# A windowed-attention and gated-MLP kernel on one core: q and k in one transfer each, heads paired two apart, other accumulator banks for the third chunk, another instruction order

## The chip, the cores and the metric

The kernel runs on one core of one Trainium2 chip. The core has TensorE (PE in the profile, with PEld for its weight loads), VectorE (DVE), ScalarE (ACT), GpSimd (POOL) and SyncE (SP), whose queue issues nearly all transfers, and 16 DMA engines that carry them. Sums of matmuls lie in eight banks of the PSUM memory, everything else on the chip in SBUF. The metric is the device time of one execution in microseconds (us).

## The reference

Four batches, eight heads, 768 positions and a head size of 64; attention sees 8 global positions and the last 96, with a bias that falls with distance. Its output, as 3072 rows of 512, goes through an MLP with 2048 hidden columns and the activation h·tanh(softplus(h)).

```
scores = scale * np.matmul(q, k.transpose(0, 1, 3, 2))
rel = pos[:, None] - pos[None, :]
is_global = pos[None, :] < int(n_global)
is_local = (rel >= 0) & (rel < int(n_local))
dist = np.where(is_global & ~is_local, float(n_local), np.abs(rel))
scores = scores - slopes[:, None, None] * dist
scores = np.where(is_global | is_local, scores, -1e9)
a = softmax(scores)
x = (a @ v), heads side by side, 3072 x 512
h = x @ w_in
g = h * np.tanh(np.where(h > 20.0, h, np.log1p(np.exp(np.minimum(h, 20.0)))))
out = g @ w_out
```

## The kernel before

The tokens are cut into 12 **chunks** of 256 (three to a batch), each chunk into two blocks of 128. The heads are worked in two sets of four, so there are 24 **groups** (two to a chunk): group G holds q and k of four heads of chunk G/2. For each group the kernel loads q (tile qr, 128 rows, 2 × 256) and the keys that the window sees (tile kr, 128 rows, 2 × 416): 64 rows for one head of a pair, 64 for the other. Attention in the first three chunks is computed in 32-bit floats (CF32 = 3). In the later ones, and in the MLP throughout, each operand is split into two 16-bit floats whose products are added.

The instructions of all engines come from one string, PROGRAM. A token is a letter and a number; the loop calls the letter's function with the number, and each engine, and each queue, runs its share of the calls in that order. A mark (') moves the operation to another engine (VectorE in place of ScalarE or of GpSimd). The letters that matter here:

- q: `load_qk`, loads of group G (L163 on). v, x: loads and copies of values (vo, vc). w: loads of weights of the MLP (wts, wr).
- s: scores (L407), one call for two pairs of heads, so group G is used by s4G and s4G+2. t: their maxima on VectorE (L421). y: exponentials on ScalarE (L430).
- P: the probabilities are turned by TensorE in the first three chunks (L460) and F copies them out (tile AT). In later chunks X turns them by a transposing transfer on SP's queue (L450).
- W: the probabilities weigh the values (L482, L486). R and what follows: the rows are normalised, turned (O, U or the transfer V) and split.
- A, S, B, C, D, E: the weights of the MLP are split into two 16-bit parts.
- i: layer 1 (L549), 8 blocks to a chunk, so i0 to i95. j, u, n, r, G, H, z, Z: its activation. o: layer 2 (L605). Q, Y: output. L, M: masks.

PSUM's eight banks go by name: two for scores (sc), two for layer 1 (ph), two for layer 2 (po0, po1) and two for the sums of weighed values (pav0, pav1). Before the change, `turn_p` puts the turned probabilities of chunk 2 in the ph banks (those of chunks 0 and 1 in po), and `weigh` puts all sums in pav.

In `load_qk` q is one transfer per group from qT, 128 rows of 2 × 256. k is two transfers of 64 rows from kd, one to each head of the pairs. In the first chunk of a batch only the last 288 of the 416 columns are loaded (144 KB each in place of 208 KB). For group 0 the second half of k is issued on ScalarE's queue, everything else on SyncE's. The tiles qr and kr have three buffers each, so the load of a group waits until the one three loads back is converted or used.

Of the kernel before, what the change touches and what calls it, by code (L numbers as in the profile page):

```python
# [114 lines left out]
def windowed(st, tc, loc):  # L115
# [47 lines left out]
    def load_qk(G):  # L163
        if G >= 2 * NC:
            return
        ci, g = divmod(G, 2)
# [5 lines left out]
        nc.sync.dma_start(qr, L.qT[b].rearrange("(a j) d s -> (j d) a s", j=2)[:, pairs, c * CH:(c + 1) * CH])  # L172
# [469 lines left out]
    def checks(i):  # L642
# [40 lines left out]
        R2 H0 P17 s18 O2 W15 W14 y16 A4 F17 z0 t19 y19 C7 t18 T2' U2 E3 E1 Z0 P16 s20 P19 C4 t20 B6 t21 y18 F19 y20 F16' D4' E4' S5' A5 B12 R3 B5 o0 P20 P18
        s22 y21 F20 S12 A12 W17 O3 S6 T3 F18 A6 A8 C5 D7' t22 U3 W19 W20 P21 i8 E7 B8 C6 C12 t23 S8' D6' y22 F21 y23 j8 D5 E6 G8 E5' C8 B13 B10 S13' W21 P23
        W18 W16 P22 F22' R4 F23 u8 n8 S10 D12 r8 A13 D8 W23 i1 i9 w16 w11 E12 E8 H8 j1 A10 u1 S9 z8' C13 G1 j9 O4 W22 A14' Z8' C10 D10' R5 o8 u9 n1 n9 r1 r9
        T4 A15 S14 A11 E10 G9 A9' D13' E13 H1 U4 B14 i2 i10 z1 B9 C14 B15 B11 H9 Z1 S11 j2 z9 C11 C9 G2 h3' Z9' j10 u10 n10 D9 D11 r10 D14 u2 n2 S15' G10
        E9' S16' C15 H10 z10' r2 D15 A16 E14 w18 w24 w22 w21 w20 w17 w25 q6 w19 w26 Z10 H2 E11' o1 o9 i3 o10 O5 B16 S18 C16 A18 z2 j3 E15 Z2 u3 A17 n3 T5
        S17 A20 S20' r3 D16' G3 A24 B18 B17 U5 E16' B20 C18 B24 C17 D17 H3 o2 i11 i16 j11 z3 S24 G11 D18' E18 i12 w28 q7 w23 u11 J16 A22 n11 r11 Z3 C20 D20
        j12 A25' B19 E17 H11 S22' G12 A19 z11 C24 Z11' o3 i4 i17 D24 B22 E24 C22 E20 S19 u12 j4 D22 u4 n4 c7 n12 G4 S25' C19 B25 a7' C25 d7' b7 o11 s24 i18
        D19 r12 J17 r4 E22' H4 N0 t24 D25' A26' H12 t25 z4' J18 y25 A21 z12 E25' l3 E19' Z12' S26' B21 B26 Z4' i13 s26 i5 o12 j13 y24 G13 u13 S21 j5 A28 o4  # L690
        i20 q9 w30 w27 S28' C21 C26 D26' E26' B23 B28 t26 A30 u5 n5 D21 C28 g25 r5 n13 B30 G5 J20' S30' g24 E21' y26 r13 A23 H5 S23' i19 i6 p25' z5 A27 C23
        J19' D23 E23' c8' C30 H13 j6 u6 D28 g26 z13 B27 p26' Z5 Z13' D30' G6 E28' E30 p24 d8 w29 X25 w31 v4 X24 q8 x3 X26 i14 o5 i21 j14 u14 n6 r6 n14 S27
        r14 G14 H6 t27 S31 a8 i7 C27 y27 J21 z6 j7 u7 D27 B29 b8 S29' E27 Z6' H14 z14 Z14 i15 s28 o13 o14 o6 n7 r7 j15 u15 a9 n15 A31' A29' B31 G7 H7 t28
        C29 C31 G15 D31' z7' Z7' r15 D29 j16 u16 j17 y28 u17 n17 n16 r16 g27 H15 g28' p28' G16 z15' t29 E29 E31 H16 Z15 z16' G17 p27' Z16' o7 s30 o15 j18
# [4 lines left out]
        z24 o23 i27 W33 W32 s38 i26 y36 n25 r25 j27 g34' p34' h5' g37 u27 Q2 j26 a12 b11 Z24' H25 G27 g36' t39 p37' z25' p36 Z25 t38 G26 y39 n27 r27 y38 u26
        X34 q12 X37 q14 X36 o24 o25 W35 s40 i28 i29 W34 W37 g39 n26 r26 p39 H27 t40 H26 z26' c12' Z26' z27' t41 l5 j28 u28 g38 n28 Z27 d12 p38 G28 r28 y40  # L700
        j29 u29 n29 X39 x5 X38 W39 o26 o27 s42 W36 W38 i30 H28 G29 y41 r29 z28 H29 a13' g40' R8 T8' g41' p41' t43 j30 c13 p40 Z28 X40 U8 b12 o28 R9 z29 V8
        u30 Z29 t42 T9 G30 y43 v6 d13 U9 i31 n30 r30 g43' V9 p43' H30 s44 X41 j31 z30' o29 u31 t45 X43 n31 G31 r31 y45 q15 H31 i32 z31' t44 Z30' Y2 b13 q13
        o30 j32 y42 g42 g45' p45' G32 h6' X45 u32 p42' i34 n32 a15' l6 y44 r32 g44' x6 s46 j34 W43 t47 W40 y47 i33 H32 X42 t46 u34 y46 Z31' z32' c14' n34
        Z32 o31 p44' j33 u33 Q3 g47' p47' W41 G34 s48 X44 G33 n33 W45 o32 r33 r34 H33 z33' g46' Z33 t49 i36 H34 t48 d14 z34 p46' y49 Z34' X46 o33 j36 y48
        G36 X47 g49' u36 p49 n36 o34 r36 a14 H36 g48' s50 i35 i37 j35 z36 G35 u35 b14 Z36 n35 t51 r35 i38 p48 y51 H35 z35' j37 t50 Z35 u37 G37 y50 W44 g51'
        W46 R10 s52 n37 W47 j38 W42 T10' o35 X49 r37 U10 H37 V10 p51' z37 t52 c15 Z37 o36 a16' v7 u38 X51 n38 R11 r38 X48 G38 o37 T11' U11 H38 V11 b15 d15'
# [188 lines left out]
```

## Time and profile before

| | us |
|---|---|
| median of 3 runs (lowest to highest) | 622.98 (621.86 to 624.29) |
| the profiled execution, its own time | 621.52 |
| the profiled execution, span of its trace | 619.7 |
| VectorE busy | 463.2 |
| ScalarE busy | 444.8 |
| GpSimd busy | 163.3 |

The costliest groups of the page (line, engine, operation, out<-in, count, busy time and mean of one, and the idle time before them with what ended it):

```profile
L549 PE MATMUL ph<-xT,wts 128*128 128x256 f16 x2304 | 263.6, 273 | 0.2 <-POOL wts L154 0.2
...
L605 PE MATMUL po<-wts,gt 128*128 128x512 f16 x1056 | 238.7, 379 | 0.8 <-DVE gt L148 0.5
```

The two layers of the MLP take 502.3 of TensorE's busy time; the rest is attention. "Busy" counts an engine's instructions only, so the wait for a transfer shows as idle time of the engine that waits, with the releaser's name behind the arrow. A transfer's row gives the time at which it was issued, and the page's list of issues the time from there to landing.

### The profile page before, as it was taken

The numbers are of one execution on the slowest core, as the hardware profiler recorded it, in microseconds if no ns is written. First come the engines' busy times: TensorE is split into PE (matmuls) and PEld (weight loads), VectorE is DVE, ScalarE is ACT, GpSimd is POOL, SyncE is SP. The second block draws the span as 40 slices with busy tenths as digits, with TensorE's granted clock in tenths as the row PEclk, the third lists the DMA queues.
The fourth block names the chain that finished last, engine by engine and source line by source line (L and its number), as shares of the span: only waits on it lengthen the run. The fifth ranks groups of instructions, "written<-read, shape, count | busy, mean of one in ns | idle before, by whom it ended". The sixth has DMA issues, their size and how long they took to land.

```text
span 619.7 us, 13567 instructions
## 1 busy us (share of the span) xinstructions
PE 603.1 (97%) x5066; PEld 417.0 (67%) x5066; DVE 463.2 (75%) x1198; ACT 444.8 (72%) x1106; POOL 163.3 (26%) x135
## 2 busy tenths in 40 slices
...
DMA  8998465235365859226357554474374344320001
GB/s 222 285 264 280 142 201 150 71 110 133 69 142 132 161 103 217 53 63 144 69 90 196 100 129 103 102 176 62 68 160 83 65 71 105 87 35 1 34 2 38
DMA packets 123014, 73.02 MB, mean 118 GB/s; under 512 B 91712, under 2 KB 112192, under 8 KB 122944
## 3 DMA queue, kind: packets, MB, share of 16 engines
q1 hardware_dynamic: 122800, 71.97, 49.8%
...
q10 hardware_dynamic: 144, 0.15, 0.1%
...
## 4 chain that ended last, share of the span: by engine, by line
PE 77%; DVE 11%; ACT 4%; issue 4%; DMA 2%; SPq 0%; POOL 0%; DVEq 0%; ACTq 0%; POOLq 0%
PE ph L549 33%; PE po L605 30%; PE sc L407 5%; PE pav L486 3%; PE pav L482 2%; DVE gf L587 2%; DVE gf L583 2%; DMA wts<-w_in 1%; DMA AT<-hl 1%; DVE ws L357 1%; PE po L460 1%; DVE A L421 1%; ACT A L430 1%; PE pav L605 1%; DVE ws L353 1%
## 5 line engine op out<-in xcount | busy, mean ns | idle before, releaser
L549 PE MATMUL ph<-xT,wts 128*128 128x256 f16 x2304 | 263.6, 273 | 0.2 <-POOL wts L154 0.2
L549 PEld LDWEIGHTS <-wts 128*128 128x128 f16 x2304 | 222.8, 98 | 35.5 <-issue 1.9
L605 PE MATMUL po<-wts,gt 128*128 128x512 f16 x1056 | 238.7, 379 | 0.8 <-DVE gt L148 0.5
L605 PEld LDWEIGHTS <-gt 128*128 128x128 f16 x1152 | 110.1, 98 | 126.8 <-issue 2.9
L154 POOL TENSOR_TENSOR gt<-gf,gt 128x512 f16<-128x512 f32 x55 | 67.5, 1229 | 278.7 <-DVE gt L148 142.7
L567 ACT ACTIVATE e<-ph 128x512 f32<-128x512 f32 x90 | 53.1, 590 | 89.9 <-PE ph L549 89.7
L430 ACT ACTIVATE A<-A,nm 128x256 f32<-128x256 f32 (+1 forms) x192 | 91.6, 478 | 29.1 <-DVE nm L421 29.1
L587 DVE CUSTOM_DVE_ANT_0 gf<-gf,u 128x512 f32<-128x512 f32 x96 | 79.5, 829 | 42.9 <-ACT u L579 41.7
L583 DVE SCALAR_TENSOR_TENSOR gf<-e,ph 128x512 f32<-128x512 f32 x90 | 61.1, 682 | 52.4 <-ACT e L567 51.3
L421 DVE CUSTOM_DVE_ANT_0 A<-sc,mb 128x256 f32<-128x256 f32 (+1 forms) x192 | 68.3, 396 | 16.9 <-PE sc L407 13.8
L154 POOL TENSOR_TENSOR hl<-A,hl 128x512 f16<-128x512 f32 (+1 forms) x36 | 44.8, 1250 | 74.2 <-DVE hl L148 31.8
L571 ACT ACTIVATE u<-e 128x512 f32<-128x512 f32 x96 | 59.9, 625 | 1.7
L579 ACT ACTIVATE u<-u 128x512 f32<-128x512 f32 x96 | 59.4, 624 | 1.8
L575 ACT ACTIVATE u<-u 128x512 f32<-128x512 f32 x96 | 59.5, 623 | 1.7
L154 POOL TENSOR_TENSOR wts<-ws,wts 128x512 f16<-128x512 f32 x20 | 25.7, 1292 | 72.1 <-ACT wts L150 37.6
L150 ACT ACTIVATE gt<-gf 128x512 f16<-128x512 f32 x44 | 27.4, 623 | 22.0 <-DVE gmax L587 22.0
L430 ACT ACTIVATION_READ_ACCUMULATOR A<-A,nm 128x1 f32 x192 | 36.0, 188 | 0.0
L486 PEld LDWEIGHTS <-AT 128*128 128x128 f16 x792 | 28.7, 98 | 7.2 <-issue 1.9
L154 DVE TENSOR_TENSOR hl<-A,hl 128x512 f16<-128x512 f32 (+1 forms) x36 | 30.0, 834 | 2.0 <-ACT hl L150 1.7
L154 DVE TENSOR_TENSOR gt<-gf,gt 128x512 f16<-128x512 f32 x41 | 28.9, 706 | 3.3 <-ACT gt L150 2.9
L407 PE MATMUL sc<-wc,ws 64*128 64x256 f16 (+1 forms) x432 | 28.2, 262 | 0.7 <-DVE nm L421 0.7
L486 PE MATMUL pav<-vo,AT 128*128 128x64 f16 x432 | 27.5, 193 | 0.0
...
## 6 DMA issues: line engine op xcount, KB each, us to landing
kr<-kd SPq DMA_DIRECT2D x32, 208.0 KB, 4.2
qr<-qT SPq DMA_DIRECT2D x24, 256.0 KB, 4.2
wts<-w_in SPq DMA_DIRECT2D x12, 512.0 KB, 8.3
wts<-w_out SPq DMA_DIRECT2D x12, 512.0 KB, 8.9
out<-ob SPq DMA_DIRECT2D x11, 512.0 KB, 3.8
vr<-v SPq DMA_DIRECT2D x9, 512.0 KB, 5.1
...
kr<-kd SPq DMA_DIRECT2D x15, 144.0 KB, 5.1
```

The costliest lines, as they stand in the source:

```text
L154: (nc.vector if other else nc.gpsimd).tensor_tensor(out, in_, high, op=ALU.subtract)
L407: nc.tensor.matmul(sc[j][:, a2, 0:w], x[half, a2, rows_], y[half, a2, col0:col0 + w], start=(n == 0), stop=(n == len(terms) - 1))
L421: nc.vector.tensor_tensor_reduce(out=A[:, j, 0:w], in0=sc[j][:, 0:w], in1=m, scale=-1.0 / (UNIT if ci < CF32 else UNIT * SQ), scalar=3.0e3 ...
L430: nc.scalar.activation(A[:, j], A[:, j], AF.Exp, bias=nm[:, h:h + 1], scale=-1.0, accum_out=rs[:, h:h + 1])
L486: nc.tensor.matmul(pav[:, cols], AT[:, (x * 2 + j) * nk + kk, :], vs[kk][:, y, cols], start=(n == 0), stop=(n == last))
L549: nc.tensor.matmul(ph[:, j, :].rearrange("p (b t) -> p b t", b=2), wv4[:, 2 * fb, x, c * P:(c + 1) * P], xT[:, :, y * NCC + c, :], start=( ...
L571: nc.scalar.activation(u, mish[m]["e"], AF.Square, bias=0.5)
L575: nc.scalar.activation(mish[m]["r"], mish[m]["u"], AF.Ln, bias=0.25 / RS, scale=1.0 / RS)
L579: nc.scalar.activation(r, r, AF.Exp, scale=-1.0)
L583: nc.vector.scalar_tensor_tensor(gf, mish[m]["e"], 0.5, mish[m]["h"], op0=ALU.add, op1=ALU.mult)
L587: nc.vector.tensor_tensor_reduce(out=gf, in0=gf, in1=mish[m]["r"], scale=SG / (SV * SW * RS), scalar=0.0, op0=ALU.mult, op1=ALU.max, accum ...
L605: nc.tensor.matmul(pos[ci][t], gt[:, x, j, t * P:(t + 1) * P], wv4[:, 2 * fb + 1, y, :], start=(fb == 0 and n == 0), stop=(fb == NFB - 1 a ...
```

## The change

1. `load_qk`: q and k of a group are each one transfer, written as a pattern of three loops: 2 half sets, 64 rows, and one run of 2 heads × 256 (or 416) columns. All 416 columns are loaded in every chunk. k of group 0 goes on ScalarE's queue. q now comes from qd, which is laid out as kd is.
2. The rows of a half set belong to heads h and h+1; a pair on TensorE's upper and lower rows is now h and h+2 (`head`).
3. The copy of the far values to vc (32 rows) is one transfer in place of two in chunks 1 and 2.
4. No mask is made on GpSimd.
5. `turn_p` puts the turned probabilities of chunk 2 in the scores' banks (sc) in place of layer 1's (ph), and `weigh` puts the sums of chunk 2 in layer 1's banks in place of pav. `turn_x32` uses sc for chunk 2.
6. PROGRAM has the same tokens in another order up to about i30 and z31, 230 us into the trace before; behind that only a few tokens move by a place or two.

```
-        pairs = slice(g * GH // 2, (g + 1) * GH // 2)
...
-        nc.sync.dma_start(qr, L.qT[b].rearrange("(a j) d s -> (j d) a s", j=2)[:, pairs, c * CH:(c + 1) * CH])
-        for j in range(2):
-            half = slice(j * D, (j + 1) * D)
-            (nc.scalar if G == 0 and j else nc.sync).dma_start(kr[half, :, o:], L.kd[ci, half].rearrange("p (a j) w -> p a j w", j=2)[:, pairs, j, o:])
+        for dst, src, w, queue in ((qr, L.qd, CH, nc.sync), (kr, L.kd, KW, nc.sync if G else nc.scalar)):
+            both = bass.AP(src.tensor, ci * P * H * w + g * GH * w, [[D * H * w + GH // 2 * w, 2], [H * w, D], [1, GH // 2 * w]])
+            queue.dma_start(dst.rearrange("p a w -> p (a w)"), both)
...
+    def head(g, a2, j):
+        return g * GH + j * (GH // 2) + a2
...
-                for t in range(2):
-                    nc.sync.dma_start(vc[NPREV:P, t], far)
+                nc.sync.dma_start(vc[NPREV:P], far.unsqueeze(1).broadcast_to([NGMAX, 2, DM]))
...
-        if other and h >= H // 2:
-            nc.gpsimd.tensor_scalar(out, in_, -L.slopes[h] * UNIT, None, op0=ALU.mult)
-        else:
-            copy(out, in_, -L.slopes[h] * UNIT, other)
+        copy(out, in_, -L.slopes[h] * UNIT, other)
...
-            h = g * GH + 2 * a2 + j
+            h = head(g, a2, j)
...
-        turn = ps.tile([P, 2, CH], F32, name="ph") if t >= 2 * 8 else ps.tile([P, DM], F32, name=f"po{t % 2}", bufs=1).rearrange("p (j t) -> p j t", j=2)
+        turn = ps.tile([P, 2, W], F32, name="sc") if t >= 2 * 8 else ps.tile([P, DM], F32, name=f"po{t % 2}", bufs=1).rearrange("p (j t) -> p j t", j=2)
...
-            pavs[ci, blk] = ps.tile([P, DM], F32, name=f"pav{blk}", bufs=1)
+            if ci == 2:
+                pavs[ci, blk] = ps.tile([P, 2, CH], F32, name="ph").rearrange("p j t -> p (j t)")
+            else:
+                pavs[ci, blk] = ps.tile([P, DM], F32, name=f"pav{blk}", bufs=1)
...
-        turn = ps.tile([P, 2, CH], F32, name="ph").rearrange("p j t -> p (j t)").rearrange("p (k t) -> p k t", t=P)
+        turn = (ps.tile([P, 2, CH], F32, name="ph") if n < 4 else ps.tile([P, 2, W], F32, name="sc")).rearrange("p j t -> p (j t)").rearrange("p (k t) -> p k t", t=P)
...
-        I0 K0 L2 K1 L4 L0 L3 v0 w2 q1 x0 s0 t1 y1 M3 P1 L1' t0 s2 B2 F1' f0 M0 M2 M1 L5 y0 A2 t3 t2 P0 W1 y3 P3 q2 w0 v1 w1 q3 x1 s4 F0' M6' M4' M7' L7' M5'
+        I0 K0 s0 w2 v0 q1 w0 x0 q2 w1 K1 L0' L1 L3 t1 M5 y1 L2' t0 L6 M2 M7 L5 M4 L7 y0 M1 M0 M3' f0 B2 A2' P1 s2 F1' S2' C2 P0 W1 t3 t2 y3 F0' P3 s4 A0'
```

What that does to the engines' orders at three places. First SyncE's queue at the start of the program; n_i is the pair of window sizes, vo and vc are values, wts weights. Before:

```order
L62 DMA n_i<-n 128x4
L172 DMA qr<-qT 128x2x256
L175 DMA kr<-kd 64x2x288
L209 DMA vo<-v 128x2x512
L322 DMA wts<-w_in 128x4x256
L172 DMA qr<-qT 128x2x256
L175 DMA kr<-kd 64x2x288 x2
L229 DMA vc<-v 96x512
```

and with the change:

```order
L62 DMA n_i<-n 128x4
L171 DMA qr<-qd 128x1x512
L317 DMA wts<-w_in 128x4x256
L208 DMA vo<-v 128x2x512
L171 DMA qr<-qd 128x1x512
L171 DMA kr<-kd 128x1x832
L317 DMA wts<-w_in 128x4x256
L228 DMA vc<-v 96x512
```

The first weights (token w2) are issued ahead of the values, q and k are one row each of 128 rows (the shape is the tile's), and a second load of weights stands ahead of the copies to vc.

Second, SyncE's queue in chunks 4 and 5, some 200 us into the trace, where q12, q14 and q15 are loaded between the transposing transfers of probabilities (AT) and of rows of x (xT). Before, with q12 and q14 as the two loads of q:

```order
L450 DMA_TRANSPOSE AT<-hl 128x8x128
L172 DMA qr<-qT 128x2x256
L175 DMA kr<-kd 64x2x288 x2
L450 DMA_TRANSPOSE AT<-hl 128x8x128
L172 DMA qr<-qT 128x2x256
L175 DMA kr<-kd 64x2x416 x2
L450 DMA_TRANSPOSE AT<-hl 128x8x128 x2
```

and with the change, with q12, q14 and q15:

```order
L445 DMA_TRANSPOSE AT<-hl 128x8x128 x2
L171 DMA qr<-qd 128x1x512
L171 DMA kr<-kd 128x1x832
L445 DMA_TRANSPOSE AT<-hl 128x8x128
L530 DMA_TRANSPOSE xT<-xhl 128x8x128
L171 DMA qr<-qd 128x1x512
L171 DMA kr<-kd 128x1x832
L208 DMA vr<-v 128x2x512
L530 DMA_TRANSPOSE xT<-xhl 128x8x128
L445 DMA_TRANSPOSE AT<-hl 128x8x128 x2
L171 DMA qr<-qd 128x1x512
L171 DMA kr<-kd 128x1x832
```

The loads of groups 12 and 14 have moved behind the transposes X39 and X38 (the first row) and X40, so that they stand close to that of group 15.

Third, VectorE ahead of the first maxima of chunk 0's second block (tile A from sc, token t3); fl are flags of the window sizes, ws and wc parts of weights. Before:

```order
L353 TENSOR_SCALAR ws_172<-wts_99 128x512
L148 TENSOR_SCALAR AT_174<-po1_159 128x256
L626 TENSOR_SCALAR fl_105<-n_f_62 1x1
L627 TENSOR_SCALAR fl_105<-n_f_62,fl_105 1x1
L628 TENSOR_SCALAR fl_105<-n_f_62,fl_105 1x1
L629 TENSOR_SCALAR fl_105<-n_f_62,fl_105 1x1
L421 ISA A_190,nm1_189<-sc_166,mb_97 128x256
```

and with the change:

```order
L627 TENSOR_SCALAR fl_105<-n_f_62,fl_105 1x1
L348 TENSOR_SCALAR ws_181<-wts_99 128x512
L148 TENSOR_SCALAR wc_183<-wts_99 128x512
L148 TENSOR_SCALAR AT_194<-po1_185 128x256
L342 TENSOR_SCALAR ws_181<-wts_99 128x512
L352 SCALAR_TENSOR_TENSOR ws_181<-wc_183,ws_181 128x512
L416 ISA A_206,nm1_205<-sc_188,mb_97 128x256
```

Three more operations on the first weights stand ahead of the maxima on VectorE, and the flags ahead of them all.

More of the change, by code (lines that the diff above doesn't have):

```diff
@@ L476, in weigh @@
         for j in range(2):
-            h = g * GH + 2 * a2 + j
+            h = head(g, a2, j)
             cols = slice(h * D, (h + 1) * D)
@@ L556, in hold_h @@
         if k < 2:
-            if k == 0:
+            if "h" not in obs:
                 obs["h"] = mt.tile([P, 2, DM], F32, name="ob", bufs=1)
@@ L683, in windowed @@
[L683 to L694, printed above, removed]
@@ L699, in windowed @@
[L699 to L706, printed above, removed]
@@ L719, in windowed @@
-        Z59' X72 W70 j61 W71 o59 u61 G61 a24 H60 g75 R17 X73 n61 r61 p75' i62 z60' T17' Z60 H61 z61' Z61 s76 j62 o60 u62 G62 n62 r62 a22 H62 W72 W73 t77 o61
-        z62 h10' Z62 U17 t76 i63 V17 y76 l10 X75 b24 o62 j63 u63 n63 g74 g76' p76 d21 G63 y77 i65 p74' g77 r63 p77 H63 X77 i64 j65 q22 z63 u65 Z63' X74 s78
-        j64 o63 u64 G64 X76 G65 n64 n65 t78 r65 y78 H65 W77 i66 r64 H64 t79 y79 z64' W75 g78' W74 Z64 Q7 s80 W76 p78 t81 i67 j66 y81 R18 u66 T18' c22 z65'
-        o64 Z65' n66 j67 G66 t80 u67 n67 U18 o65 b22 r67 V18 r66 G67 g79' X78 p79' H66 i68 X79 z66' g81' Z66 H67 v11 d22' p81 W78 j68 o66 u68 n68 X81 z67 Y7
@@ L723, in windowed @@
-        s82 x10 W79 t82 a23 i69 y82 Z67' r68 g82' G68 y80 t83 o67 H68 R19 z68 j69 Z68 T19' u69 s84 n69 G69 o68 r69 U19 g80 b23 V19 y83 p82' p80' X82 i70 t85
-        y85 t84 X80 H69 c24 g85' z69' i71 j70 Z69 u70 G70 h11' n70 r70 o69 H70 j71 z70' g83' Z70 p85 s86 o70 p83 X83 t86 y86 d24' W81 u71 W82 G71 X85 i74
-        n71 c23' y84 d23 r71 i73 j74 u74 G74 H71 n74 t87 r74 i72 g84' j73 z71' p84 u73 n73 Z71 X84 r73 g86 s88 j72 p86 o71 t88 u72 H74 y87 G73 g87 t89 y88
-        p87 W84 H73 W80 W83 z74' n72 W85 X87 r72 Z74' i75 G72 X86 g88' H72 p88' s90 j75 X88 i76 u75 t91 t90 R20 W87 z73' z72 y89 Z72 Q8 o72 T20 Z73 y91 n75
@@ new lines, in windowed @@
+        F3' L4 y2 t4 t5 y5 y4 P2 W3 s6 F2' S0' M6' B0 t6 w3 v1 q3 x1 P4 W2 P5 W0 t7 A1' S1' C0 B1 F4 y6 F5 y7 P6 s8 W4 P7 W5 t8 t9 R0 C1 F6 y8 F7 y9 D2 W6
+        s10 P8 P9 W7 O0 t11 t10 D1 F8' A3' E1' R1 y11 y10 F9 T0 D0 S3 E2 E0 s12 W8 P11 O1 W9 P10 w7 w13 q4 w24 w8 w6 q5 w12 v2 w4 w5 w11 w10 x2 w14 t13 t12
+        T1' B3 U1 U0 y13 F11 y12 F10 s14 P13 i0 P12 A7 F13 S13 t14 S7' B7 C3 B13 t15 C7 F12' y14 y15 W13 s16 W12 P15 P14 W11 W10 j0 G0 S6 u0 A13 n0 r0 D7'
+        D3' t17 R2 H0 z0' t16 B6 A6 F15 F14 y17 y16 O2 W15 W14 P17 P16 E3 E7 Z0 F17 T2 A4 F16 R3 O3 o0 s20 T3 C13 C6 B4 S4' U2 C4 U3 D6 D4 i8 E4' t20 D13'
@@ new lines, in windowed @@
+        S28 S27' C27 Z13' B28 C28 i6 i20 w30 q8 X25 w31 q9 w29 X24 X26 J20' j6 n5 j16 A30 c8 r5 u6 D27 S30' B30 G6 g27' d8' H5 C30 a8' b8 D28' z5' o13 i14
+        i21 s28 j14 n6 u14 n14 Z5 E27 u16 r6 D30 r14 n16 G14 J21' r16 t29 E28' H6 y29 z6' H14 Z6 E30 o5 i19 i7 z14 S31 t28 J19 y28 S29 G16 B29 H16 z16 j7
+        j17 u7 n7 r7 u17 n17 o6 s30 i15 Z16 B31 A29' Z14' C29 D29' g28' G7 E29' g29' A31' a9' r17 C31 H7 z7 j15 D31 u15 c9 n15 r15 G17 Z7' E31 o14 o7 p27'
+        b9 G15 H17 H15 z15' d9 t30 Z15' p28' Q0 j19 j18 u18 y30 u19 o16 o15 X27 x3 Y0 n18 r18 Q1 n19 r19 p29' z17' Z17' G18 t31 H18 z18' Z18 g30' G19 H19
@@ new lines, in windowed @@
+        j20 a10 y31 u20 n20 j21 u21 r20 z19' l4 Z19' c10' G20 G21 p30 o17 W25 s32 W26 W24 o18 i22 q10 X28 X29 X30 W28 W29 W27 t32 H20 g31 n21 z20 r21 p31'
+        R6 H21 z21' Z21' t33 T6 Z20 U6 q11 X31 o19 i23 W30 W31 s34 o20 o21 j22 R7 T7' j23 u23 u22 n22 y32 r22 U7 g32' G22 t34 d10 p32 b10 t35 n23 y33 y34
+        g34 g33 r23 G23 p34' H23 z23' H22 z22' Z22 p33 V6 V7 X33 Y1 X32 x4 v5 X34 i24 s36 i25 j24 u24 G24 t36 Z23 n24 j25 u25 n25 r24 y36 y35 r25 G25 t37
+        H24 c11' o22 o23 s38 i26 W32 i27 W33 g35 Q2 j26 j27 u26 d11 n26 a11 r26 y37 g37 z24' p35' g36' t39 H25 z25' p36 Z24 a12' Z25' t38 G26 G27 H26 c12'
@@ new lines, in windowed @@
+        h5 u27 y38 y39 z26' d12' l5 b11 Z26' p37 X36 X35 X37 x5 o24 o25 i28 W35 s40 W36 W34 o26 W37 i29 g39 j28 u28 g38 n27 r27 H27 z27 n28 p39 p38 Z27 X39
+        X38 q12 r28 t40 G28 b12 y40 j29 t41 R8 H28 z28 g40' p40' G29 T8 u29 Z28' o27 W39 s42 W38 i30 o28 U8 t43 c13' y41 a13 n29 r29 j30 H29 z29' u30 g41'
+        Z29 p41 R9 X40 V8 q14 v6 T9 d13 y43 t42 i31 G30 n30 U9 r30 g43' V9 p43' s44 H30 j31 X41 z30' o29 u31 t45 n31 X43 G31 r31 y45 H31 q15 i32 z31' t44 Y2
+        Z30' b13 q13 o30 j32 y42 g42 g45' p45' G32 X45 h6' u32 p42' i34 n32 a15' l6 y44 r32 g44' x6 s46 j34 W43 t47 W40 y47 i33 H32 X42 t46 u34 y46 Z31'
@@ new lines, in windowed @@
+        z32' c14' n34 Z32 o31 p44' j33 u33 Q3 g47' p47' W41 G34 s48 X44 G33 n33 W45 o32 r33 r34 H33 z33' g46' Z33 t49 i36 H34 t48 d14 z34 p46' y49 Z34' X46
+        o33 j36 y48 G36 X47 g49' u36 p49 n36 o34 r36 a14 H36 g48' s50 i35 i37 j35 z36 G35 u35 b14 Z36 n35 t51 r35 i38 p48 y51 H35 z35' j37 t50 Z35 u37 G37
+        y50 W44 g51' W46 R10 s52 n37 W47 j38 W42 T10' o35 X49 r37 U10 H37 V10 p51' z37 t52 c15 Z37 o36 a16' v7 u38 X51 n38 R11 r38 X48 G38 o37 T11' U11 H38
+        V11 b15 d15' i39 t53 y53 z38' g50' b16 p50 s54 j39 i40 u39 G39 Z38 X50 y52 n39 q16 r39 H39 W49 Y3 o38 z39' t55 Z39 y55 c16 o39 j40 d16 g53 G40 g52
@@ new lines, in windowed @@
+        X64 y68 G55 p67' y69 X67 s70 z54 W66 t71 c20 Z54 i56 v9 g68' g69 H55 p69' z55 o54 Z55 j56 u56 d19 n56 h9' r56 d20 o55 G56 t70 y70 b21 p68' Q6 i57
+        H56 X68 g70 z56 X69 W67 j57 s72 i58 u57 t72 G57 n57 Z56' r57 b20 y71 H57 W64 j58 W68 z57' i59 g71 G58 Z57 u58 l9 p70 p71' W69 j59 o56 u59 X70 n58
+        t73 G59 n59 X71 r58 R16 y72 o57 Y6 T16' g72 y73 x9 g73' H58 q21 s74 z58 i60 Z58 t75 v10 p73' q23 p72 o58 j60 u60 G60 c21' n60 t74 r59 y75 i61 H59
+        U16 r60 z59' V16 y74 Z59' X72 W70 j61 W71 o59 u61 G61 X73 a24 H60 g75 R17 n61 r61 p75' i62 z60' T17' Z60 H61 z61' Z61 s76 j62 o60 u62 G62 n62 r62
@@ new lines, in windowed @@
+        a22 H62 W72 W73 t77 o61 z62 h10' Z62 U17 t76 i63 V17 y76 l10 X75 b24 o62 j63 u63 n63 g74 g76' p76 d21 G63 y77 i65 p74' g77 r63 p77 H63 X77 i64 j65
+        q22 z63 u65 Z63' X74 s78 j64 X76 o63 u64 G64 G65 n64 n65 t78 r65 y78 H65 W77 i66 r64 H64 t79 y79 z64' W75 g78' W74 Z64 Q7 s80 W76 p78 t81 i67 j66
+        y81 R18 u66 T18' c22 z65' o64 Z65' n66 j67 G66 t80 u67 n67 U18 o65 b22 r67 V18 r66 G67 g79' X78 p79' H66 i68 X79 z66' g81' Z66 H67 v11 d22' p81 W78
+        j68 o66 u68 n68 X81 z67 Y7 s82 x10 W79 t82 a23 i69 y82 Z67' r68 g82' G68 y80 t83 o67 H68 R19 z68 j69 Z68 T19' u69 s84 n69 G69 o68 r69 U19 g80 b23
```

58 lines of the change are left out of this document (28 added, 30 removed).

## The prediction

> **What bounds the kernel now.** I read the busy table first, then the chain of work that ended last, then the busy slices, then the stretches, and last the transfers. The page of the profile:
>
> ```profile
> PE 603.1 (97%) x5066; PEld 417.0 (67%) x5066; DVE 463.2 (75%) x1198; ACT 444.8 (72%) x1106; POOL 163.3 (26%) x135
> ...
> DMA  8998465235365859226357554474374344320001
> ...
> q1 hardware_dynamic: 122800, 71.97, 49.8%
> ...
> PE 77%; DVE 11%; ACT 4%; issue 4%; DMA 2%; SPq 0%; POOL 0%; DVEq 0%; ACTq 0%; POOLq 0%
> ```
>
> TensorE is busy for 603.1 of 619.7 us, and it is most of the chain. So the kernel runs at the length of its matmuls, and a change can save at most the 16.6 us in which TensorE stands still. It can lose any amount, if something makes TensorE wait. The DMA row says where that could come from: in the first 60 us, and again in three or four bursts, the 16 engines are nearly full. The stretches show it in numbers (columns: stretch, length, busy time of PE, PEld, DVE, ACT and POOL, granted clock, DMA share, GB/s):
>
> ```profile
> 0.00:20.00 20.00, 11.85 (x78) 8.77 (x80) 12.52 (x61) 11.90 (x43) 4.82 (x12) 1.00 0.92 252
> 80.00:100.00 20.00, 19.20 (x138) 13.26 (x137) 19.09 (x31) 16.76 (x34) 9.28 (x7) 1.00 0.47 145
> 160.00:180.00 20.00, 19.24 (x190) 12.15 (x189) 19.26 (x48) 18.48 (x50) 6.17 (x5) 1.00 0.61 125
> 180.00:200.00 20.00, 19.11 (x133) 11.85 (x130) 17.78 (x45) 12.90 (x34) 3.96 (x3) 1.00 0.56 128
> ...
> 20.00:40.00 20.00, 20.00 (x170) 17.19 (x169) 18.60 (x68) 19.08 (x60) 4.49 (x4) 1.00 1.07 258
> 21.00:25.00 4.00, 4.00 (x35) 3.56 (x36) 3.81 (x18) 3.68 (x13) 0.00 (x0) 1.00 1.06 243
> 48.00:50.00 2.00, 2.00 (x13) 1.10 (x12) 1.97 (x7) 2.00 (x8) 0.00 (x0) 1.00 1.04 385
> 53.00:55.00 2.00, 2.00 (x20) 2.00 (x19) 2.00 (x8) 1.76 (x4) 1.17 (x1) 1.00 0.95 359
> ```
>
> Half of TensorE's idle time lies before 20 us (20 − 11.85 = 8.15). After that it never waits long, with VectorE busy nine tenths of the time beside it. Where the DMA share is 1, all 16 engines move 243 to 385 GB/s together. One engine's rate is therefore 385/(16 × 1.04) = 23.1 GB/s at 48 to 50 us, 359/(16 × 0.95) = 23.6 at 53 to 55, and 243/(16 × 1.06) = 14.3 at 21 to 25, where the 64-row halves of k travel.
>
> **The loads of q and k.** Which transfers there are, with their size and the time from issue to landing:
>
> ```profile
> kr<-kd SPq DMA_DIRECT2D x32, 208.0 KB, 4.2
> qr<-qT SPq DMA_DIRECT2D x24, 256.0 KB, 4.2
> wts<-w_in SPq DMA_DIRECT2D x12, 512.0 KB, 8.3
> ...
> kr<-kd SPq DMA_DIRECT2D x15, 144.0 KB, 5.1
> ...
> vc<-vc SPq DMA_DIRECT2D x12, 64.0 KB, 2.6
> ```
>
> 256 KB in 4.2 us is 62 GB/s with the latency counted in, more than two engines' worth: before, a load of q is spread widely. Every transfer of before starts its pattern with a loop over 32, 64, 96 or 128 rows. The new pattern of q and of k starts with a loop over 2 (two half sets of heads), with 64 rows below it, and ends in one run of 2 or 3.25 KB. How many engines share such a transfer is the **unknown of this change**, and no row of before shows it. The ends are 16 engines, as for all transfers so far, and two, one to each step of the outer loop. An even share needs a loop that it can be cut along, and the outermost loop is the one that all the transfers of before have with a count of 16 or more. I take the cut along it, so two engines, and the same two each time.
>
> The Trainium skill, page "DMA: Bandwidth & Descriptors", section "Why a DMA increments its semaphore by 16 and not by 1", has a rule for this: a transfer goes over the largest number of engines, up to 16, that divides the slowest loop (of size above 1) of both patterns, and the hardware queues use the lowest-numbered engines. Here that is two, always the same; the trace neither confirms nor denies it. It speaks against this change and for my choice.
>
> With two engines a group's 256 + 416 KB = 688,128 bytes take 344,064/23.1 = **14.9 us**. At 14.3 GB/s they would take 24.1.
>
> **The start.** Where the first groups are needed (columns: start, length, engine, line, operation):
>
> ```profile
> 1.20 0.42 SPq L172 DMA_DIRECT2D qr<-qT  x1
> ...
> 6.06 1.22 PE L407 MATMUL sc<-kr,qr 64*128 64x128 f32 x8 [6.06 <-DMA kr<-kd]
> ...
> 7.11 0.43 DVE L279 SCALAR_TENSOR_TENSOR e<-e 128x256 f32<-128x256 f32 x1
> ...
> 7.46 0.28 DVE L421 CUSTOM_DVE_ANT_0 A<-sc,mb 128x128 f32<-128x128 f32 x1
> ...
> 10.75 0.55 DVE L353 TENSOR_SCALAR ws<-wts 128x512 uint16<-128x512 uint16 x1 [2.14 <-DMA wts<-w_in]
> ...
> 45.48 1.14 PE L407 MATMUL sc<-kr,qr 64*128 64x256 f32 x8
> ```
>
> The last row is token s20, the first scores of group 5. Groups 0 to 5 are 6 × 14.9 = 89.4 us on each of the two engines. On SP's queue eleven transfers of 512 KB and the transfers for x0 and x1 (about 0.75 MB) stand ahead of group 5 or among them. Spread over 16 engines, each of the eleven takes 524,288/16/23.1 = 1.42 us, and all of this 15.6 + 2.1 = 17.7 us. With 3 us until the first bytes flow, group 5 is there at 89.4 + 17.7 + 3 = 110.1 us, and s20 is **64.6 us** late. Everything on TensorE stands in program order behind it. The new order puts some matmuls ahead of s20 and takes others away, which could give back 2 or 3 us; I leave that out. The first scores come at 17 to 20 us instead of 6.06.
>
> **Later.** After the start there are 18 groups for some 500 us, so single loads of 14.9 us hide, and bursts don't:
>
> ```profile
> 220.02 5.30 SPq L450 DMA_TRANSPOSE AT<-hl  x2
> ...
> 235.75 0.58 SPq L172 DMA_DIRECT2D qr<-qT  x1
> ...
> 238.49 0.41 SPq L172 DMA_DIRECT2D qr<-qT  x1
> ...
> 402.36 0.72 SPq L172 DMA_DIRECT2D qr<-qT  x1
> ...
> 405.15 0.47 SPq L172 DMA_DIRECT2D qr<-qT  x1
> ...
> 431.46 0.58 SPq L172 DMA_DIRECT2D qr<-qT  x1
> ```
>
> ```profile
> 250.81 0.26 PE L486 MATMUL pav<-vc,AT 128*128 128x64 f16 x3
> ...
> 419.93 0.51 PE L486 MATMUL pav<-vo,AT 128*128 128x64 f16 x12
> ...
> 439.92 0.25 PE L486 MATMUL pav<-vc,AT 128*128 128x64 f16 x3
> ...
> 484.85 0.83 PE L407 MATMUL sc<-wc,ws 64*128 64x256 f16 x12
> ```
>
> In the new order q12 and q14 are issued behind the transposes X39 and X38 (the row at 220.02, until 225.3), with q15 and q13 close behind (235.75 and 238.49) and then X45. Four groups are 59.6 us, so X45 comes out of the engines at 225.3 + 59.6 = 284.9, and its weighing W45 stood at 250.81: **+34.1**. Groups 21 and 23 (402.36 and 405.15) push X72 to 402.36 + 29.8 = 432.2, against W72 at 419.93: **+12.2**. Group 22 pushes X74 to 431.46 + 14.9 = 446.4, against W74 at 439.92: **+6.4**. If the transposes pass the loads, only the scores of group 13 are late, by 14 us.
>
> A check without any single wait: queue q1 holds each engine for 0.498 × 619.7 = 309 us. About 41 of these (15.1 MB/16/23.1) are q and k; in their place come 24 × 14.9 = 358. The two engines then have 626 us of work, more than the whole span, and up to group 22's load:
>
> ```profile
> 0.00:431.50 431.50, 420.90 (x3572) 295.25 (x3573) 356.49 (x925) 328.60 (x833) 120.76 (x101) 1.00 0.59 141
> ```
>
> 0.59 × 431.5 = 255, less 41, plus 358, is 572 us before q22 has landed, while s88, its first user, stood at 484.85. So +87 at the least if the two engines hold all of it, and some +75 if q and k held 53 instead of 41.
>
> **The other parts.** *Fewer issues:* 48 for q and k instead of 72, each near 0.6 us of SP by the rows above; SP isn't waited for, so nothing, either way. *Heads h and h+2 paired:* the same instructions on other columns, nothing. *Banks:* chunk 2's probabilities now turn in the scores' banks and its sums lie in layer 1's. That frees the two sum banks earlier for layer 2 of chunk 1. In return the next scores wait for the copy out of the bank:
>
> ```profile
> L148 DVE TENSOR_SCALAR gt<-gf 128x512 f16<-128x512 f32 x15 | 7.2, 481 | 0.3
> ...
> L148 DVE TENSOR_SCALAR AT<-po 128x512 f32<-128x512 f32 x6 | 4.1, 684 | 0.8 <-PE po L460 0.8
> ```
>
> Eight turns by 0.684 us, all uncovered, would be +5.5. The best case is that the gaps in 80 to 100, 160 to 180 and 180 to 200 us (0.80 + 0.76 + 0.89) go: −2.4. I take 0, since TensorE is at 20.00 of 20.00 in the stretch beside them. *The order of weights and masks:* masks leave POOL, and three more operations on weights (near 0.5 us each by the gt row: some 1.5 us) now stand before the second block's maxima on VectorE, which in return need not wait 2.14 us for w2. That cancels to within 1 us.
>
> **Rivals.**
> 1. *Sixteen engines, nothing gained.* The loads take 4 to 8 us as before. Having q and k sooner buys nothing, as VectorE makes the masks until 7.54 (7.11 + 0.43) and takes its first maximum at 7.46 already. VectorE, at 0.89 to 0.99 of its time, sets the pace until 200 us. 621.5, or with its extra conversions up to 624. For it: all transfers of before do spread. Chance 0.10.
> 2. *Sixteen engines and faster.* One mechanism: VectorE's wait of 2.14 us at 10.75 goes, and the freed banks fill the 2.4 us of gaps: 621.5 − 2.1 − 2.4 = 617. It decides where the loads of group 0 land before 6 us; then VectorE's queue, not the transfers, sets the start. Chance 0.09.
> 3. *A small split, but on changing engines,* so that groups run beside each other. Only the first scores wait, 17 to 20 instead of 6.06, and the bursts vanish: 621.5 + 12 = 634. Nothing in the profile says that the engines change. Chance 0.05.
>
> **How the numbers follow.** The sum against the profiled execution's own time (621.5; the median of the runs is 623.0, so 1.5 more): 621.5 + 64.6 + 34.1 + 12.2 + 6.4 = **739 us**, chance 0.76. Its bounds: if the transposes pass the loads, 621.5 + 64.6 + 14 = 700. At 14.3 GB/s a group takes 24.1: +120 at the start, +71, +31 and +16 later, 859. The new rows are long, so I stay near 23 GB/s, and the forecast's own range is 690 to 830. The range that holds 8 in 10 must reach down to rival 1, since above 690 alone lies too little: 620 to 820. Half a per cent (3.1 us) is about what a measurement of this kernel can tell from no change. Faster by more than that 0.09 (rival 2), within it 0.10 (rival 1), slower 0.81 (the forecast and rival 3).
>
> **What would show it.** Right: the first scores start at 15 us or later, released by a DMA of k; q and k need 10 us or more to land each; the DMA share falls far below 0.9 in the first 60 us while TensorE waits; the scores at 45 us come after 90; near 250 us TensorE waits for AT from a DMA. Wrong at its root: q and k land within 5 us at the start. Wrong in size: the time of one group isn't near 15 us, or the weights and transposes land on time beside the loads, so that the later terms are missing. The banks are wrong if TensorE waits in the scores of chunk 2 for VectorE's copy of a turn.

## The result and the profile after

The changed kernel takes 820.61 us (median of 6 runs, the lowest 818.45), the kernel before, on the same chip, 622.42. The ratio is 1.317 with a 95% interval of 1.313 to 1.321: slower, by 198 us where 117 were forecast. The time lies inside the forecast's own range and 0.6 us above the end of the wider one. (One of the six runs took 3583.71 us, which nothing recorded explains; the ratio leaves it out.)

The page of the profile after, the lines that answer to those of before:

```profile
PE 651.1 (80%) x5066; PEld 440.9 (54%) x5066; DVE 460.7 (56%) x1209; ACT 443.8 (54%) x1100; POOL 158.1 (19%) x130
...
PEclk9756879999989699777998988999979899999999
DMA  2243375336928854937447898774937534523000
...
q1 hardware_dynamic: 115582, 72.73, 54.4%
...
PE 46%; DMA 31%; SPq 8%; DVE 8%; ACT 3%; issue 3%; POOL 1%; DVEq 0%; ACTq 0%; POOLq 0%
PE ph L547 20%; PE po L603 19%; DMA AT<-hl 12%; DMA kr<-kd 5%; DMA wts<-w_out 4%; PE sc L402 3%; SPq L171 3%; DMA wr<-w_out 2%; PE pav L484 2%; DMA qr<-qd 2%; DMA out<-ob 2%; SPq L208 2%; DMA xT<-xhl 2%; SPq L317 1%; DMA vc<-vo 1%
```

The chain that was TensorE's for 77% is now 46% TensorE and 31% transfers, and the largest of these are not q and k (7%) but the transposes of probabilities (AT, 12%) that travel on the same engines. TensorE stands still for 816.7 − 651.1 = 165.6 us where it was 16.6. Its busy time rose as well, by 48 us with the same matmuls: the row PEclk shows a lower granted clock in many slices. So of the 197 us by which the span grew, 149 are waits and 48 are slower matmuls.

How many engines share a load is read where nothing else is in flight. Stretches of the changed kernel (columns as before: the last three are granted clock, DMA share and GB/s):

```profile
26.00:28.00 2.00, 0.51 (x4) 0.21 (x2) 0.26 (x1) 1.20 (x6) 0.00 (x0) 1.00 0.15 53
28.00:30.00 2.00, 0.00 (x0) 0.00 (x0) 0.00 (x0) 0.00 (x0) 0.00 (x0) 0.86 0.55 161
30.00:32.00 2.00, 0.00 (x0) 0.00 (x0) 0.00 (x0) 0.00 (x0) 0.00 (x0) 0.50 0.13 50
32.00:34.00 2.00, 0.00 (x0) 0.00 (x0) 0.00 (x0) 0.00 (x0) 0.00 (x0) 0.50 0.13 52
...
42.00:44.00 2.00, 2.00 (x16) 1.60 (x13) 1.39 (x8) 0.87 (x4) 0.00 (x0) 0.73 1.03 300
44.00:46.00 2.00, 1.04 (x10) 0.81 (x8) 0.08 (x2) 2.00 (x8) 0.00 (x0) 1.00 1.01 271
...
50.00:55.00 5.00, 1.08 (x6) 1.00 (x8) 0.00 (x0) 0.00 (x0) 0.00 (x0) 0.50 0.13 51
...
375.00:380.00 5.00, 0.00 (x0) 0.00 (x0) 0.00 (x0) 2.06 (x5) 0.00 (x0) 0.76 2.62 62
```

0.13 of 16 engines is 2.1: two engines, at 51/2 = 25.5 GB/s each. A group alone takes 688,128/51 = 13.5 us. They are the same two for both queues: in 8 to 11 us q of group 0 comes on SyncE's queue (q1) and k on ScalarE's (q10), and together they have a share of 0.131.

```profile
q10 hardware_dynamic: 29, 0.10, 8.0%
q1 hardware_dynamic: 29, 0.06, 5.1%
```

The rule of the Trainium skill, page "DMA: Bandwidth & Descriptors", section "Why a DMA increments its semaphore by 16 and not by 1", that the slowest loop of the pattern sets the number of engines, agrees with these shares.

TensorE's scores at the start (a row each for groups 0 to 5, with the idle time before it and its releaser):

```profile
19.06 1.23 PE L402 MATMUL sc<-kr,qr 64*128 64x128 f32 x8 [19.06 <-DMA qr<-qd]
...
36.06 1.22 PE L402 MATMUL sc<-kr,qr 64*128 64x128 f32 x8 [9.54 <-DMA kr<-kd]
...
53.91 2.08 PE L402 MATMUL sc<-kr,qr 64*128 64x256 f32 x8 [8.87 <-DMA kr<-kd]
73.11 2.08 PE L402 MATMUL sc<-kr,qr 64*128 64x256 f32 x8 [7.85 <-issue]
92.04 2.08 PE L402 MATMUL sc<-kr,qr 64*128 64x256 f32 x8 [5.49 <-DMA kr<-kd]
...
111.67 1.19 PE L402 MATMUL sc<-kr,qr 64*128 64x256 f32 x2 [5.13 <-DMA kr<-kd]
```

One group every 18.5 us, and group 5 at 111.67 where 110.1 was forecast. The rest of the loss comes later; two of its largest waits, with the transposes as releasers:

```profile
355.90 5.03 PE L547 MATMUL ph<-xT,wts 128*128 128x256 f16 x24 [8.39 <-DMA xT<-xhl]
388.59 0.34 PE L484 MATMUL pav<-vc,AT 128*128 128x64 f16 x3 [14.88 <-DMA AT<-hl]
```

### The profile page after: what moved, and what is told of

Its sections match the earlier page's. It is cut to its first block, busy times and chain, and to the rows that moved or that the text cites. A ratio compares the mean times of both kernels' runs of the same rounds, so it can differ in the third digit from the quotient of the medians.

```text
span 816.7 us, 13519 instructions
## 1 busy us (share of the span) xinstructions
PE 651.1 (80%) x5066; PEld 440.9 (54%) x5066; DVE 460.7 (56%) x1209; ACT 443.8 (54%) x1100; POOL 158.1 (19%) x130
## 4 chain that ended last, share of the span: by engine, by line
PE 46%; DMA 31%; SPq 8%; DVE 8%; ACT 3%; issue 3%; POOL 1%; DVEq 0%; ACTq 0%; POOLq 0%
PE ph L547 20%; PE po L603 19%; DMA AT<-hl 12%; DMA kr<-kd 5%; DMA wts<-w_out 4%; PE sc L402 3%; SPq L171 3%; DMA wr<-w_out 2%; PE pav L484 2%; DMA qr<-qd 2%; DMA out<-ob 2%; SPq L208 2%; DMA xT<-xhl 2%; SPq L317 1%; DMA vc<-vo 1%
## 5 line engine op out<-in xcount | busy, mean ns | idle before, releaser
L547 PE MATMUL ph<-xT,wts 128*128 128x256 f16 x2304 | 272.5, 278 | 10.7 <-DMA xT<-xhl 8.4
L603 PE MATMUL po<-wts,gt 128*128 128x512 f16 x1056 | 254.2, 396 | 22.9 <-DVE gt L148 10.9
L547 PEld LDWEIGHTS <-wts 128*128 128x128 f16 x2304 | 226.9, 100 | 51.6 <-DMA xT<-xhl 8.9
L603 PEld LDWEIGHTS <-gt 128*128 128x128 f16 x1152 | 113.6, 101 | 161.0 <-issue 29.6
L565 ACT ACTIVATE e<-ph 128x512 f32<-128x512 f32 x90 | 53.0, 590 | 122.4 <-PE ph L547 122.4
L402 PE MATMUL sc<-kr,qr 64*128 64x256 f32 (+1 forms) x96 | 22.6, 573 | 64.6 <-DMA kr<-kd 29.0
L484 PE MATMUL pav<-vc,AT 128*128 128x64 f16 x360 | 25.7, 197 | 44.3 <-DMA AT<-hl 32.5
L402 PEld LDWEIGHTS sc<-kr,qr 64*128 64x128 f32 x96 | 13.4, 287 | 69.3 <-issue 61.6
L150 ACT ACTIVATE gt<-gf 128x512 f16<-128x512 f32 x39 | 24.3, 624 | 37.5 <-DVE gmax L585 37.5
L148 DVE TENSOR_SCALAR hl<-A 128x512 f16<-128x512 f32 (+1 forms) x41 | 19.9, 485 | 39.4 <-DMA AT<-hl 32.8
L154 DVE TENSOR_TENSOR hl<-A,hl 128x512 f16<-128x512 f32 (+1 forms) x36 | 26.8, 752 | 21.7 <-ACT hl L150 21.5
```

What stands on the lines that cost most here:

```text
L154: (nc.vector if other else nc.gpsimd).tensor_tensor(out, in_, high, op=ALU.subtract)
L402: nc.tensor.matmul(sc[j][:, a2, 0:w], x[half, a2, rows_], y[half, a2, col0:col0 + w], start=(n == 0), stop=(n == len(terms) - 1))
L484: nc.tensor.matmul(pav[:, cols], AT[:, (x * 2 + j) * nk + kk, :], vs[kk][:, y, cols], start=(n == 0), stop=(n == last))
L547: nc.tensor.matmul(ph[:, j, :].rearrange("p (b t) -> p b t", b=2), wv4[:, 2 * fb, x, c * P:(c + 1) * P], xT[:, :, y * NCC + c, :], start=( ...
L603: nc.tensor.matmul(pos[ci][t], gt[:, x, j, t * P:(t + 1) * P], wv4[:, 2 * fb + 1, y, :], start=(fb == 0 and n == 0), stop=(fb == NFB - 1 a ...
```

## The experiments

Runs without an interval were executed once. Before's own median was 621.7 to 623.8 us on the three chips that were used, so a difference of 2 us between two single runs says nothing.

**First, whether the loads are the cause.** The changed kernel with each load in two halves of 64 rows, so that the pattern starts with a loop over 64:

```
+ for j in range(2):
+     queue.dma_start(flat[j * D:(j + 1) * D], bass.AP(src.tensor,
+         ci * P * H * w + g * GH * w + j * (D * H * w + GH // 2 * w), [[H * w, D], [1, GH // 2 * w]]))
```

> The changed kernel with each load of q and k cut into two transfers of 64 rows, so that the pattern begins with a loop over 64 rows. Same bytes, order, banks and head pairs. Theory (a transfer is shared out along its outermost loop, two engines for a loop of 2): the first scores start near 6 us instead of 19.06, the DMA share reaches 0.9 in the first 20 us, and the time is 617 to 626 us. Rival (the order and the banks cost the time, the loads only follow): it stays above 780 us.

630.43 us: ratio to before 1.0132, interval 1.0104 to 1.0159. The two-step loads are 190 of the 198 us. But the kernel is still 8 us above before, which neither theory had. Its page, the wait that stands out (VectorE, then TensorE) and two stretches there:

```profile
PE 608.8 (97%) x5066; PEld 421.5 (67%) x5066; DVE 461.3 (74%) x1209; ACT 442.9 (71%) x1100; POOL 158.7 (25%) x130
```

```profile
205.65 0.43 DVE L148 TENSOR_SCALAR hl<-A 128x512 f16<-128x512 f32 x1 [5.57 <-DMA AT<-hl]
...
208.98 6.61 PE L608 MATMUL po<-wts,gt 128*128 128x512 f16 x22 [2.79 <-POOL gt L154]
```

```profile
205.00:210.00 5.00, 2.21 (x23) 1.16 (x22) 4.31 (x10) 4.50 (x12) 2.71 (x2) 1.00 0.30 54
210.00:215.00 5.00, 5.00 (x18) 1.91 (x16) 5.00 (x13) 4.06 (x11) 1.94 (x2) 0.66 0.74 158
```

VectorE waits 5.57 us until a transpose frees its buffer, TensorE waits 2.79 behind it, and then runs at 0.66 of its clock.

**The loads alone in the old order.** Before's order and banks, with the new `load_qk`, the pairing of heads, and L1 and L2, L5 and L6, M1 and M2, M5 and M6 exchanged in PROGRAM:

```
+ both = bass.AP(src.tensor, ..., [[D * H * w + GH // 2 * w, 2], [H * w, D], [1, GH // 2 * w]])
+ queue.dma_start(dst.rearrange("p a w -> p (a w)"), both)
...
+ h = head(g, a2, j)
```

> The kernel before with nothing changed but the loads of q and k, now one transfer each with the loop over 2 outermost, and with that the pairing of heads h and h+2 and the masks in the order that it needs. Theory: 790 to 850 us, as the loads are the whole loss; stretches with only q and k in flight show a DMA share near 0.13. Rival (order and banks): below 650 us.

810.92 us. The loads cost as much in the old order: +189. With nothing else in flight the share is 0.13 here too:

```profile
30.00:35.00 5.00, 0.00 (x0) 0.00 (x0) 0.00 (x0) 0.00 (x0) 0.00 (x0) 1.00 0.13 52
```

**The two parts of the program.** The loop over 2 kept for some groups, halves of 64 rows for the others (`if G < 6:` and `if G >= 6:` ahead of the two forms):

> The changed kernel with the loop over 2 outermost for groups 0 to 5 only; groups 6 to 23 are loaded in halves of 64 rows. If the start costs what was predicted (64.6 us) and nothing later: 680 to 692 us, with the scores of group 5 near 110 us. Rival: the late start lets transfers and VectorE get ahead, part of it is won back: 650 to 675.

698.37 us: the start costs 698.4 − 630.4 = 67.9 against the form with halves throughout. The scores of group 5 start at 112.35. The time is 6 us above the range expected; that range had left out the 8 us of the order.

> The opposite: groups 0 to 5 in halves of 64 rows, the loop over 2 outermost for groups 6 to 23. By the terms of the prediction (34.1 + 12.2 + 6.4) 675 us. If instead each single group delays the transposes behind it, not the bursts alone, the loss of the changed kernel after its scores of group 5 (198 less 66) returns: 745 to 765 us.

753.32 us, 122.9 above the halves: the second answer. The terms of the prediction hold less than half of the late loss.

**Order and banks apart from the loads.** Before's order and banks with the loads of the first experiment:

> The kernel before with q and k in halves of 64 rows, all columns, heads h and h+2 paired and the masks in the order that it needs: the loads of the first experiment in the order and the banks of before. If order and banks are what leaves the first experiment 8 us above before: 620 to 625 us. If its loads are (four issues a group, 1 MB more): 628 to 633.

623.2 us, ratio 1.0005, interval 0.9978 to 1.0033. So four issues a group and 1 MB more cost nothing that can be measured. The 8 us belong to the rest of the change: the new order with its banks, the masks moved off GpSimd and the single copy to vc. No run parts these; either order is written for its own banks.

**What a late load does.** Only q of the late groups on two engines (`if G >= 6 and src is L.qd:`):

> The changed kernel, with the loop over 2 outermost for q of groups 6 to 23 only; k of these groups and everything of groups 0 to 5 in halves of 64 rows. The two engines are held for 256 of 672 KB a group, some 5 us in place of 13.5. If every load delays what is behind it by its own length: 630 + 123 x 0.38 = 677 us. If transposes and scores have slack of 5 us or more and only longer loads or bursts count: 630 to 645.

655.22 us, +24.8: between the two answers. A hold of 5 us costs 1.4 us a group on average, one of 13.5 us costs 122.9/18 = 6.8. So there is slack, but less than 5 us in some places: TensorE waits for a transfer for 1.0 to 5.2 us in four places after 180 us.

The late two-step loads issued from ScalarE's queue (`nc.scalar.dma_start(flat, both)`):

> As the experiment with the late groups on two engines (753 us), but those transfers are issued from ScalarE's queue; SyncE keeps the transposes, weights and outputs. If the loss is the wait behind the loads in SyncE's own queue, in order, most of it goes: 640 to 690 us. If the two engines' time is shared whoever issues, 730 to 760.

755.8 us: no relief. The chain that ended last, with all loads on SyncE's queue (753.32 us) and with the late ones on ScalarE's:

```profile
PE 54%; DMA 29%; DVE 7%; issue 3%; ACT 3%; SPq 3%; POOL 1%; POOLq 0%; DVEq 0%; ACTq 0%
```

```profile
PE 39%; DMA 31%; DVE 11%; ACT 8%; ACTq 4%; issue 3%; POOL 2%; SPq 0%; POOLq 0%; DVEq 0%
```

Transfers hold as much of the chain on either queue, though in the second run SyncE's queue has none of the late loads left. So the transposes wait mainly for the two engines, which a transfer from either queue needs. The separation isn't clean: ScalarE pays for its issues here, 4% of the chain or some 30 us, and a gain of that size could hide behind it.

All loads from GpSimd's queue (`nc.gpsimd.dma_start`):

> The changed kernel with all its loads of q and k, loop over 2 outermost, issued from GpSimd's queue. Rival of the prediction (a small split on changing engines): the loads of several groups run beside each other, the first scores come at 15 to 20 us and the time is 630 to 680 us. If the same two engines serve them on this queue too: 780 us or more.

769.29 us, between the two. The first scores came at 26.58 us, later than with SyncE's queue. The whole run on this queue (q0), the time in which k lands, and the queue in 230 to 235 us:

```profile
q0 software_dynamic: 25344, 16.69, 10.6%
...
kr<-kd POOLq DMA_DIRECT2D x24, 416.0 KB, 16.5
```

```profile
q0 software_dynamic: 87, 0.43, 24.3%
```

In these 5 us q and k move at 86 GB/s on a share of 0.243, which is four engines and not two. So on this queue the engines do change and loads run beside each other, the mechanism of rival 3. (Of the 25,344 packets 22,272 hold 8 bytes or fewer; the data go in 3,072 packets of 4 and 6.5 KB.) But the rival's 634 us isn't there: k takes 16.5 us to land, and transfers hold 28% of the chain. What makes up the 769 wasn't taken apart.

**Which late groups.** The loop over 2 for groups 12 to 15, then for 6 to 11 and 16 to 20, then for 21 to 23, halves for the rest:

> All loads of q and k in halves of 64 rows (630.4 us), except groups 12 to 15, which keep the loop over 2 outermost. By the term of the prediction for this burst (34.1): 664 us, with W45 late by as much. If the term was right by chance only: below 645 or above 685.

664.63 us: +34.2, where the term has 34.1. The waits of TensorE behind the burst:

```profile
243.94 1.78 PE L407 MATMUL sc<-wc,ws 64*128 64x256 f16 x12 [6.38 <-DVE nm L421]
258.85 5.30 PE L552 MATMUL ph<-xT,wts 128*128 128x256 f16 x24 [9.64 <-DMA xT<-xhl]
291.86 0.34 PE L489 MATMUL pav<-vc,AT 128*128 128x64 f16 x3 [14.77 <-DMA AT<-hl]
```

The last row is W45. In the first experiment it stands at 256.46, so it is 35.4 us late, as expected:

```profile
256.46 0.26 PE L489 MATMUL pav<-vc,AT 128*128 128x64 f16 x3
```

That the numbers agree to a tenth is luck: the forecast moved W45 from 250.81 to 284.9, and the one lies 5.7 and the other 7.0 us later here. And the loss isn't taken at W45 at once, as the sum had it, but in three steps. The first step isn't a matter of transposes. In the chain that ended last (start and length of each link) it comes from k of group 12 itself, which VectorE turns into 16-bit floats (wc) in its own order and waits for:

```profile
223.27 16.27 DMA kr<-kd
...
239.56 0.46 DVE L148 TENSOR_SCALAR wc<-kr 128x576 f16<-128x576 f32 x1 [9.10 <-DMA kr<-kd]
```

> As before, but the loop over 2 for groups 6 to 11 and 16 to 20 only, which the prediction costed at nothing (single loads hide). If they do hide: 630 to 636 us. If each delays the transposes and copies issued behind it, what the late groups cost beyond the bursts (123 less about 51) returns: 690 to 710.

685.47 us: +55.0, where the prediction had nothing. The longest transfers in the chain that ended last, each issued right behind a load of q and k, or behind another transfer that was:

```profile
142.68 19.42 DMA wr<-w_out
...
185.41 11.16 DMA AT<-hl
...
198.02 14.13 DMA AT<-hl
...
323.07 16.67 DMA out<-ob
...
376.24 13.03 DMA vc<-vc
```

In the first experiment no link of this kind is longer than 5.3 us. Two of the largest waits of TensorE, which come from the last two links:

```profile
340.57 5.10 PE L608 MATMUL po<-wts,gt 128*128 128x512 f16 x12 [6.39 <-ACT ob L621]
...
389.41 0.32 PE L489 MATMUL pav<-vc,AT 128*128 128x64 f16 x3 [11.77 <-DMA vc<-vc]
```

```profile
339.83 0.60 ACT L621 ACTIVATE ob<-po 128x512 f32<-128x512 f32 x1 [10.15 <-DMA out<-ob]
```

The second waits for a copy of values to vc that was issued behind a load. The first waits for ScalarE, which is to empty the bank of layer 2 (the last row) and waits 10.15 us for the one output buffer: its store was issued at 323.07, right behind q and k, and took until 339.8.

> As before, but the loop over 2 for groups 21 to 23 only. By the prediction (12.2 + 6.4): 649 us. By the lateness that the run with all late groups shows there (about 6 at W72 and 12 at W74): 648.

663.58 us: +33.2, more than either number. SyncE's queue, TensorE's two largest waits there, and ScalarE ahead of the first of them:

```profile
417.23 2.23 SPq L173 DMA_DIRECT2D qr<-qd  x1
...
423.95 17.48 SPq L535 DMA_TRANSPOSE xT<-xhl  x1
```

```profile
438.75 1.04 PE L608 MATMUL po<-wts,gt 128*128 128x512 f16 x2 [11.06 <-DVE gt L148]
...
479.34 0.34 PE L489 MATMUL pav<-vc,AT 128*128 128x64 f16 x3 [10.21 <-DMA AT<-hl]
```

```profile
436.48 0.63 ACT L150 ACTIVATE ws<-qr 128x512 f16<-128x512 f32 x1 [13.76 <-DMA qr<-qd]
```

The issue of the transpose of x took 17.48 us behind groups 21 and 23, where it took 1.26 before (the row at 409.78 of before, of the same token). But the first wait of TensorE comes from the load itself: ScalarE turns q of group 23 into 16-bit floats (ws) in its own order and waits 13.76 us for it, VectorE waits for ScalarE and TensorE for VectorE. The second wait is that for a transpose behind group 22.

**The 8 us of the order.** One token moved in the first experiment:

```
- Y1 X32 x4 v5 X34 i24
+ Y1 X32 X34 x4 v5 i24
```

> The first experiment (halves of 64 rows, 630.4 us) with one token moved: the transpose X34 ahead of x4 and v5 on SyncE's queue (four copies and a load, some 3.5 us of issues). There VectorE waited 5.57 us for a buffer that this transpose frees, and TensorE's clock fell behind it. If SyncE's order at that place costs what the first experiment loses: 622 to 626 us. If the loss is spread over the order: 628 to 632.

626.74 us, ratio 1.006, interval 1.0025 to 1.0094: between the two ranges expected. Against before on the same chip the excess falls from 1.32% to 0.60%, so some 4.5 of the 8 us hang on the place of that one transpose. Where the rest lies isn't shown. No kernel here beats the one before.

## Why the prediction was right, and where its sizes were off

| term | forecast | measured (run less 630.4) |
|---|---|---|
| start, groups 0 to 5 | 64.6 | 67.9 |
| burst, groups 12 to 15 | 34.1 | 34.2 |
| groups 21 to 23 | 12.2 + 6.4 | 33.2 |
| single late groups | 0 | 55.0 |
| order, banks, masks, copy (630.4 less 622.2) | 0 | 8.2 |
| sum | 117.3 | 198.5 |

The measured sum is the whole loss (820.6 − 622.4 = 198.2), and the three late parts, 122.4, are what the run with all of them lost (122.9). So the parts add up within what single runs can tell, some 2 us each, and no large one is missing.

*What bounds the kernel* held: TensorE's matmuls in one order, 16.6 us to win and any amount to lose. *Two engines, the same each time* held on SyncE's and ScalarE's queues; the first two experiments show it from both sides. (The release of the first scores came from q, not from k as its sign had it.) *14.9 us a group* was near: 13.5 alone. *The start* held to 1.6 us at the scores of group 5 (111.67 against 110.1), and in part by luck. At 13.5 us a group the six loads are 81 us and not 89.4, so everything else took some 10 us more than the 17.7 + 3 of the sum. The engines weren't idle meanwhile, since in no stretch of 5 us up to there was the DMA share below 0.13; which of the other transfers took the time isn't separated. The queue's issues grew as well:

```profile
2.44 8.45 SPq L208 DMA_DIRECT2D vo<-v  x1
10.93 3.30 SPq L171 DMA_DIRECT2D qr<-qd  x1
14.28 3.82 SPq L171 DMA_DIRECT2D kr<-kd  x1
```

Before, these issues took 0.58, 0.51 and, in two halves, 1.68 us.

The measured 67.9 also holds a cost of the banks that the prediction had named as a sign, for VectorE's copies, and put at nothing. The scores of group 5 stop in the middle until ScalarE has copied a turn out of their bank (the changed kernel; 5.04 us in the run with the start alone):

```profile
117.77 2.07 PE L402 MATMUL sc<-kr,qr 64*128 64x256 f32 x6 [4.92 <-ACT AT L150]
```

ScalarE itself had waited 12.53 us for weights there. In the first experiment TensorE has no such wait.

The step that failed is "single loads of 14.9 us hide, and bursts don't". It looked at the scores, which have their q and k a chunk ahead, and not at what is issued behind a load: a transpose, a copy to vc, an output or a load of weights needs the two engines as well, and in several places it is wanted sooner than it then lands. That is the 55.0 us. The same step makes groups 21 to 23 too cheap (33.2 for 18.6): the sum followed two weighings, and left out that ScalarE turns q into 16-bit floats well ahead of the scores and stands still until q lands. The 700 us that the prediction named for transposes that pass the loads is excluded, too.

*The other parts at nothing* failed by 8.2 us: the new order keeps TensorE busy in 80 to 100 and 160 to 200 us, as its best case had it (20.00, 20.00 and 19.92 of 20 in the first experiment), but lays X34 behind five other transfers near 200 us, which is some half of it. The sum had no term for the granted clock either. It is part of the rows of the table, not beside them: of the late groups' 122.9 us, 638.2 − 608.8 = 29.4 are matmuls that took longer, by the busy times of the two runs. (In its check by queue q1, q and k of before are 15,104 KB or 15.5 MB, 42 us and not 41; that changes nothing.)

Rivals 1 and 2 fell with the first experiment and its reverse. Rival 1 would have been near the truth for 64-row halves in the old order (623.2), rival 2 for none: the earlier start (first scores at 5.56 us in place of 6.06) was given back within 20 us: the fourth scores stand at 18.41 in place of 16.33. Rival 3 has its engines right for GpSimd's queue and its time for none.
